# Attention and feed-forward in one kernel: a shorter lag of the exponentials, exponentials over two banks, and another order of the last matmuls

## The chip, the cores and the metric

The kernel runs on one core of a Trainium2 chip. The metric is the device time of one execution in microseconds. Five engines work side by side, each through its own list of instructions in order: TensorE (PE), ScalarE (ACT), VectorE (DVE), GpSimd (POOL) and SyncE (SP, which here issues the DMAs). PE writes its results to PSUM, which has eight banks of 512 fp32 values per partition; ACT and DVE read them there.

## The reference

A pre-LayerNorm block for 2048 tokens of 512 channels: attention with 32 heads of 16 channels, then a gated feed-forward network of 1792 channels.

```python
def _A_ref(x, wqkv, wo):
    qkv = ((x @ wqkv).reshape(B, S, 3, H, Dh)).transpose(2, 0, 3, 1, 4)
    q, k, v = qkv[0], qkv[1], qkv[2]
    scores = jnp.einsum("bhqd,bhkd->bhqk", q, k) * (Dh ** -0.5)
    p = _softmax(scores, axis=-1)
    o = jnp.einsum("bhqk,bhkd->bhqd", p, v)
    return o.transpose(0, 2, 1, 3).reshape(B, S, D) @ wo

def _B_ref(x, w_gate, w_up, w_down):
    return (_gelu(x @ w_gate) * (x @ w_up)) @ w_down

x = A_x
h = x + _A_ref(_layernorm(x), A_wqkv, A_wo)
h2 = h + _B_ref(_layernorm(h), B_w_gate, B_w_up, B_w_down)
```

Inputs and output are bf16, S = 2048, D = 512, H = 32, Dh = 16, F = 1792.

## The kernel before

**Units and steps.** Attention is cut into 64 units. A unit is one group of 256 query tokens (`gi`, 0 to 7) and one slot of four heads (`slot`, 0 to 7); the units of one token group follow each other, so a group lasts 8 units. A unit has 16 steps, and the main loop of the kernel (L1293) counts steps in `tick`. Each unit is gone through twice.

**First pass (p1): maxima.** `p1_pair` (L787) makes, in each step, the scores of 128 queries against 512 keys for two heads: two matmuls of 512 columns (L797) into two neighbouring PSUM banks. The pairs of banks alternate between 0, 1 and 2, 3 (for the first `DOUBLES` = 20 steps there are three pairs). `p1_consume` (L803) reduces both banks to maxima with one instruction on DVE, 128x2 from 128x1024 (L806). POOL combines the maxima of a unit: `negm_part` after steps 8 and 12 (L817 to L824), `negm_pre` after step 15 (L832 to L840), which writes the negated maximum in three bf16 pieces into ST. `negm_post` issues a DMA that transposes ST into STG (L846) and, `ADDX` = 4 steps later, lets POOL add STG to the unit's part of Q (L851): K has rows of ones, so the second pass gets score minus maximum out of the matmul.

**Second pass (p2): exponentials.** It begins `P2_START` = 16 + `LAGX` steps after the first pass of the same unit. `p2_tile` (L860) makes the transposed scores, 128 keys by 256 queries, two matmuls of 256 columns into one bank (L867), for two heads a step. `p2_consume` (L872) lets ACT take the exponential of the bank (128x512 fp32, L879) into one tile of a ring of 34 bf16 tiles, which lie in three areas (PTM 23, PTE 4, PTG 7). The second pass and the work below share banks 4 to 7, which `Banks` hands out. In one step the matmuls of the first pass and the first tile of the second form a group on PE: all waits of the group stand at its first instruction (`group_begin`, `group_end`, L124 to L147), so that the next maximum's matmuls also wait for what the tile waits for.

**Dense work.** Everything else on PE is a list of small items (`Dense`, L510) that gives the loop one piece in each step: projections to Q, K and V, the product with V (`item_pv`, L893), transposes and normalisation of its result (`item_ofin`; POOL takes the reciprocal with a power, L928, and multiplies, L932), the output projection (`item_oproj`, L994), the second LayerNorm (sums by ACT with L1005 and L1012, the rest on POOL, L1022 to L1036), and the feed-forward network (`item_gate`, `item_up`, `item_down`). Gate and up results are copied out of PSUM by ACT (`evac_act`, L641; by DVE, L630, once there are no maxima left); the gelu is a chain of POOL steps around a tanh on ACT (`gelu_chain`, L1045: L1062, L1063, L1064, tanh L1055, L1060, L1061, then L1114). POOL work goes through `PoolStream` (L594), which gives POOL a budget of about 1.19 us a step and holds costly operations back in some steps. Where a step has less dense work than two matmuls of 512 columns, `dummy` (L1283) fills it with matmuls whose result nobody reads.

**Steps without maxima.** After step 1023 the second pass still has 16 + `LAGX` steps, 24 here. They are taken two at a time: four tiles, each with its exponential, then dense work or dummies up to `FILL_2` = 4 units of 512 columns. The last token group's first three quarters of the output projection (`tail_a`, `tail_a2`) are made in these steps. Then `tail_b` (L1227) normalises the last unit (`tail_norm`, `tail_onT`), finishes the projection (L1237), takes the LayerNorm on DVE (L1240 to L1251), transposes (`tail_hnT`, L1213) and runs the last feed-forward block. `fill(n)` (L1176) puts n units of dense work or dummies on PE where a chain of other engines runs; `FILL_LN` is the one behind the LayerNorm. The down projections of the group before the last wait until then (`startable`, L504).

The scheduling is all done when the program is built: on the chip each engine only runs its list and waits on semaphores.

Of the kernel before, what the change touches and what calls it, by code (L numbers as in the profile page):

```python
# [223 lines left out]
LAGX = 8  # L224
PAUSE = 1
DOUBLES = 20
FILL_2 = 4
FILL_LN = 16
# [5 lines left out]
def bass_sequential_preLN__mha_block__geglu_ffn__prompt_kernel(nc, A_x, A_wqkv, A_wo, B_x, B_w_gate, B_w_up, B_w_down, out):  # L234
    dbg = None
    with ExitStack() as es:
# [264 lines left out]
        def startable(it, room):  # L501
            if it[0] is item_gate and par_busy[it[1][1] % 2] and room < 10:
                return False
            if it[0] is item_down and it[1][0] == GL - 1 and not force[0]:  # L504
                return False
            if it[0] is item_down and it[1][1] == 0 and not force[0]:
                return not gut_left.get(it[1][0], 0) and dense.now >= gut_last.get(it[1][0], 0) + 1
            return it[0] is not item_projT or not (qks_busy.get(("a", qk_n[0] % 4)) or qks_busy.get(("b", qk_n[0] % 2)))

        class Dense:  # L510
# [17 lines left out]
            def _start(self, item):  # L528
                genfn, a, est, nb = item
                if self.single:  # L530
# [63 lines left out]
        class PoolStream:  # L594
# [23 lines left out]
        ticking = [False]  # L618
        pool = PoolStream()
# [158 lines left out]
        for fn_ in qk_late:  # L778
            fn_()
        early = {0: [lambda: stats_dve(12), c2_rest], 1: [lambda: stats_dve(13), lambda: stats_dve(14), lambda: stats_act(15)], 2: [c2_dve, c3_rest],  # L780
                 5: [c3_act], 9: [lambda: w_order("q", 1, "act")], 11: [lambda: w_order("k", 1, "act")], 16: [lambda: w_order("q", 2, "act")],
                 18: [lambda: w_order("k", 2, "act")], 20: [lambda: w_order("q", 3, "act")], 22: [lambda: w_order("k", 3, "act")]}
# [59 lines left out]
        def negm_post(ui):  # L842
# [17 lines left out]
        def p2_tile(ui, j, gp, jj):  # L860
# [3 lines left out]
            m, g, b = j // 2, 2 * gp + jj, banks.take()  # L864
# [5 lines left out]
            return (b, m, g)  # L870

# [173 lines left out]
        def gelu_chain(par, dE):  # L1045
# [4 lines left out]
            def later(n):  # L1050
                if not force[0] and act_lag[0] > LAG_OP + 0.1 * n:
# [95 lines left out]
        def tail_a(b):  # L1147
# [9 lines left out]
            dense.add(tail_a2, front=True, est=4, not_before=dense.now + 2)  # L1157
            return 1

        def tail_a2(b):  # L1160
            gp = GL % 2
            for k in range(2):
                for hc in range(3):
                    P.op("pe", lambda e, k=k, hc=hc: e.matmul(pbank[:, k, :], OnT[:, k, hc, :], wo_sb[:, hc, :], start=(hc == 0), stop=False),
                         reads=[("OHa", 0), "wo"], writes=[("pb", k)], sig=False)
                    if hc == 1:
                        yield 2
                P.op("pe", lambda e, k=k: e.matmul(pbank[:, k, :], ident[:], g_h(GL, k), start=False, stop=False),
                     reads=["ident", ("h", gp, k)], writes=[("pb", k)], sig=(k == 1))
                if k == 0:  # L1170
                    yield 2
            a_done[0] = True
            return 2
        a_done = [False]
# [118 lines left out]
        while True:  # L1293
# [5 lines left out]
            if tick == P2_START - 4:  # L1299
# [107 lines left out]
```

## Time and profile before

| | |
|---|---|
| median of three runs | 1243.11 us (1242.97 to 1243.45) |
| profiled execution | 1243.15 us |
| its span, first to last instruction | 1241.40 us |
| granted clock of TensorE, mean | 0.997 |
| maxima (L806) | 1024, first starts at 14.66 us, last ends at 1184.92 us |
| exponentials (L879) | 2048 of 128x512, first starts at 46.46 us, last ends at 1211.31 us |
| first gate matmul of the last feed-forward block | 1219.97 us |

Busy time counts an engine from the start to the end of its instructions; where instructions of one engine overlap by their start and end, their mean duration is longer than the pitch at which they follow each other. A row of the timeline has the start, the time from the first start to the last end, engine, line, operation, output and inputs, shape and how many instructions are merged in it; in brackets stands the idle time before it and what ended that. "PEld" is the loading of weights on PE.

### The profile page before, as it was taken

The numbers are of one execution on the slowest core, as the hardware profiler recorded it, in microseconds if no ns is written. First come the engines' busy times: TensorE is split into PE (matmuls) and PEld (weight loads), VectorE is DVE, ScalarE is ACT, GpSimd is POOL, SyncE is SP. The second block draws the span as 40 slices with busy tenths as digits, with TensorE's granted clock in tenths as the row PEclk, the third lists the DMA queues.
The fourth block names the chain that finished last, engine by engine and source line by source line (L and its number), as shares of the span: only waits on it lengthen the run. The fifth ranks groups of instructions, "written<-read, shape, count | busy, mean of one in ns | idle before, by whom it ended". The sixth has DMA issues, their size and how long they took to land.

```text
span 1241.4 us, 31438 instructions
## 1 busy us (share of the span) xinstructions
PE 1137.8 (92%) x12680; PEld 437.8 (35%) x12680; DVE 1189.8 (96%) x1088; ACT 1199.9 (97%) x2464; POOL 764.3 (62%) x1540
## 2 busy tenths in 40 slices
PE   7999888899999999999999998999999999999998
PEld 3333222233333333333333333333333333333335
DVE  8999999999999999999999999999999999999923
ACT  7899999999999999999999999999999999999992
POOL 8647774467746765376645777367654766547760
PEclk9999999999999999999999999999999999999989
DMA  5101004300010000100010000100002000100000
GB/s 151 31 22 28 24 19 130 89 6 3 6 31 12 6 6 6 38 5 6 4 27 18 4 6 6 27 17 6 6 4 40 6 4 6 27 19 3 6 13 18
DMA packets 50800, 27.45 MB, mean 22 GB/s; under 512 B 36064, under 2 KB 49632, under 8 KB 50656
## 3 DMA queue, kind: packets, MB, share of 16 engines
q1 hardware_dynamic: 50656, 25.45, 8.0%
q8 instruction: 101, 1.65, 0.5%
q14 instruction: 43, 0.35, 0.1%
HBM read 11.80 MB, written 2.10 MB: 11 GB/s over the span
## 4 chain that ended last, share of the span: by engine, by line
DVE 58%; ACT 30%; PE 9%; POOL 2%; issue 1%; DMA 0%
DVE PM L806 57%; ACT PTM L879 17%; ACT PTG L879 5%; ACT PTE L879 3%; PE pbank L1122 2%; PE pbank L867 2%; PE pbank L797 1%; ACT th_sb L1055 1%; PE pbank L1072 1%; ACT g_sb L641 1%; ACT OnT L1012 1%; ACT u_sb L641 1%; PE pbank L739 1%; PE pbank L998 1%; PE pbank L676 1%
## 5 line engine op out<-in xcount | busy, mean ns | idle before, releaser
L806 DVE TENSOR_REDUCE PM<-pbank 128x2 f32<-128x1024 f32 x1024 | 1162.4, 1224 | 5.3 <-PE pbank L867 2.8
L879 ACT ACTIVATE PTM<-pbank 128x512 bf16<-128x512 f32 x1388 | 737.0, 669 | 4.7
L867 PE MATMUL pbank<-QT,KT 32*128 32x256 bf16 x4096 | 498.2, 273 | 9.7 <-ACT PTM L879 4.4
L797 PE MATMUL pbank<-KT,QT 32*128 32x512 bf16 x2048 | 394.2, 382 | 46.4 <-DVE PM L806 23.6
L1285 PE MATMUL pbank<-ones_bf,ident 128*128 128x512 bf16 x794 | 245.3, 384 | 28.1 <-ACT PTM L879 3.2
L797 PEld LDWEIGHTS pbank<-KT,QT 32*128 32x128 bf16 x2048 | 104.5, 91 | 392.7 <-DVE PM L806 170.3
L879 ACT ACTIVATE PTG<-pbank 128x512 bf16<-128x512 f32 x420 | 228.2, 660 | 1.1 <-PE pbank L867 0.3
L867 PEld LDWEIGHTS pbank<-QT,KT 32*128 32x128 bf16 x4096 | 164.5, 92 | 65.7 <-ACT PTM L879 36.8
L879 ACT ACTIVATE PTE<-pbank 128x512 bf16<-128x512 f32 x240 | 137.7, 667 | 1.9 <-PE pbank L867 1.1
L893 PE MATMUL pbank<-PTM,VA 128*17 128x256 bf16 x2776 | 125.8, 274 | 2.7 <-ACT PTM L879 1.2
L832 POOL TENSOR_TENSOR MX<-PM,MX 128x8 f32<-128x8 f32 x64 | 12.9, 202 | 163.9 <-DVE PM L806 163.9
L1285 PEld LDWEIGHTS pbank<-ones_bf,ident 128*128 128x128 bf16 x794 | 47.6, 97 | 131.4 <-ACT PTM L879 83.8
L928 POOL TENSOR_TENSOR LINV<-OAT,negone 128x16 f32<-128x16 f32 (+1 forms) x32 | 92.7, 2896 | 0.0
L893 PEld LDWEIGHTS pbank<-PTM,VA 128*17 128x17 bf16 x2776 | 60.1, 89 | 46.9 <-issue 29.1
L821 POOL TENSOR_TENSOR MX<-PM,MX 128x8 f32<-128x8 f32 x64 | 13.0, 203 | 101.5 <-DVE PM L806 101.5
L1072 PE MATMUL pbank<-hnT_l,wu_sb 128*128 128x256 bf16 x448 | 67.1, 276 | 3.1 <-ACT PTM L879 0.2
L1072 PE MATMUL pbank<-hnT_l,wg_sb 128*128 128x256 bf16 x448 | 66.9, 275 | 2.5
L1114 POOL TENSOR_TENSOR GUT<-th_sb,u_sb 128x512 bf16<-128x512 f32 x49 | 62.2, 1270 | 5.1 <-DVE u_sb L630 3.0
L1061 POOL TENSOR_TENSOR th_sb<-th_sb,g_sb 128x512 f32<-128x512 f32 x49 | 62.1, 1268 | 4.1
L1064 POOL TENSOR_TENSOR th_sb<-th_sb,g_sb 128x512 f32<-128x512 f32 x49 | 62.1, 1268 | 3.1
L1062 POOL TENSOR_TENSOR th_sb<-g_sb 128x512 f32<-128x512 f32 x49 | 51.0, 1041 | 18.8 <-ACT g_sb L641 18.8
L1122 PE MATMUL pbank<-wd_sb,GUT 128*128 128x512 bf16 x224 | 60.5, 382 | 0.6 <-ACT PTM L879 0.2
(149 smaller groups left out, 1077.3 us busy)
## 6 DMA issues: line engine op xcount, KB each, us to landing
QKS<-QKS SPq DMA_DIRECT2D x27, 112.0 KB, 2.2
x_sb<-in_A_x_dram SPq DMA_DIRECT2D x4, 512.0 KB, 5.6
xres<-in_A_x_dram SPq DMA_DIRECT2D x16, 128.0 KB, 2.2
out_dram<-out_sb SPq DMA_DIRECT2D x16, 128.0 KB, 1.8
wg_sb<-in_B_w_gate_dram SPq DMA_DIRECT2D x4, 448.0 KB, 5.0
wu_sb<-in_B_w_up_dram SPq DMA_DIRECT2D x4, 448.0 KB, 4.0
wd_sb<-in_B_w_down_dram SPq DMA_DIRECT2D x3, 512.0 KB, 6.4
STG<-ST SPq DMA_TRANSPOSE x64, 2.3
```

The source lines that it names most:

```text
L797: P.op("pe", lambda e, g=g, b=b: e.matmul(pbank[:, b, :], QT[32 * g:32 * g + 32, c, slot, 128 * qt:128 * qt + 128], KT[32 * g:32 * g + 32, ...
L806: P.op("dve", lambda e: e.tensor_reduce(out=PM[:, par, qt, kc, g:g + 2], in_=pbank[:, b:b + 2, :], axis=AX.X, op=ALU.max), reads=[("pb", b ...
L867: P.op("pe", lambda e, kt=kt, i=i: e.matmul(pbank[:, b, 256 * i:256 * i + 256], KT[32 * g:32 * g + 32, slot, 128 * kt:128 * kt + 128], QT[ ...
L879: P.op("act", lambda e, b=b, pi=pi: e.activation(out=PTt(pi), in_=pbank[:, b, :], func=ACT.Exp), reads=[("pb", b)], writes=[("PT", pi)], e ...
L893: P.op("pe", lambda e, g=g, kt=kt, pi=pi, i=i: e.matmul(pbank[32 * g:32 * g + 17, b, 0:256], VA[:, kt, 4 * slot + g, :], PTt(pi)[:, 256 * ...
L928: P.op("pool", lambda e: e.tensor_tensor(out=li, in0=oat4[:, :, :, 16], in1=negone[:, 0:8 * ns].rearrange("p (q h) -> p q h", q=2), op=ALU ...
L1061: o(1.27, lambda e: e.tensor_tensor(out=ts_, in0=ts_, in1=gs, op=ALU.mult), [("th", par), ("g", par)])], then=done)
L1064: o(1.27, lambda e: e.tensor_tensor(out=ts_, in0=ts_, in1=gs, op=ALU.mult), [("th", par), ("g", par)])], then=lambda: defer(TANH_LAG, lamb ...
L1072: P.op("pe", lambda e, dc=dc, fc=fc, i=i: e.matmul(pbank[:, b, 256 * i:256 * i + 256], w[:, dc, 128 * fc:128 * fc + 128], hT[:, dc, :], st ...
L1114: P.op("pool", lambda e: e.tensor_tensor(out=o_ap, in0=shp(ts_), in1=shp(us), op=ALU.mult), reads=[("th", par), ("u", par)], writes=o_keys ...
L1122: P.op("pe", lambda e: e.matmul(pbank[:, b, :], GUT[:, fc, 128 * k:128 * k + 128], wd_sb[:, fc, :], start=first, stop=last), reads=[("GUT" ...
L1285: P.op("pe", lambda e: e.matmul(pbank[:, b, :], ident[:], ones_bf[:, 0:512], start=True, stop=True), reads=["ident", "ones_bf"], writes=[( ...
```

## The change

- `LAGX` goes from 8 to 6: the second pass of a unit begins 22 steps after its first pass instead of 24. The weight reorderings of the projections (`w_order`) are put at steps 13, 15, 17 and 19 instead of 16, 18, 20 and 22, and the single-bank mode of the dense work begins at step `DOUBLES`, which is 20 before and after.
- The steps without maxima use three fixed pairs of neighbouring banks, and `p2_pair` takes one exponential of 128x1024 over both banks where the two ring tiles are neighbours in one area, and two of 128x512 where not. `FILL_2` goes from 4 to 5.
- POOL's multiplication by the reciprocal (L932) is held back in steps 1 and 2 of a unit while an add into Q is due; the tanh of the gelu chain waits longer for ACT to catch up, and waits while a gate or up item is in progress.
- The first down projection of the group before the last may start inside the loop.
- `tail_a2` is no longer an item of the dense work: its two halves stand in `tail_b`, in place of two fills of 3. `FILL_LN` goes from 16 to 13.

```diff
-LAGX = 8
+LAGX = 6
-FILL_2 = 4
-FILL_LN = 16
+FILL_2 = 5
+FILL_LN = 13
...
-            if it[0] is item_down and it[1][0] == GL - 1 and not force[0]:
+            if it[0] is item_down and it[1] == (GL - 1, 1) and not force[0]:
...
+                    if not flush and add_due[0] and qkv_over[0] and self.q[0][1].__name__ == 'mul' and dense.now % 16 in (1, 2):
+                        break
...
+            add_due[0] = True
             def add():
+                add_due[0] = False
                 pool.spend(0.7)
...
+        def p2_pair(ui, tiles):
+            pis = []
+            for (b, m, g) in tiles:
+                pi = pt_n[0] % NPT; pt_n[0] += 1
+                assert pi not in pt_busy, "PT ring too small"
+                pt_busy.add(pi)
+                pt_of[(ui, m, g)] = pi
+                pis.append(pi)
+            (b0, b1), (q0, q1) = [t[0] for t in tiles], pis
+            assert b1 == b0 + 1
+            if q1 == q0 + 1 and pt_tiles[q0][0] is pt_tiles[q1][0]:
+                o_ap = pt_tiles[q0][0][:, pt_tiles[q0][1]:pt_tiles[q0][1] + 2, :]
+                P.op("act", lambda e: e.activation(out=o_ap, in_=pbank[:, b0:b0 + 2, :], func=ACT.Exp), reads=[("pb", b0), ("pb", b1)], writes=[("PT", q0), ("PT", q1)])
+            else:
+                for b, pi in ((b0, q0), (b1, q1)):
+                    P.op("act", lambda e, b=b, pi=pi: e.activation(out=PTt(pi), in_=pbank[:, b, :], func=ACT.Exp), reads=[("pb", b)], writes=[("PT", pi)])
...
-                if not force[0] and act_lag[0] > LAG_OP + 0.1 * n:
+                if not force[0] and (act_lag[0] > LAG_OP + 0.02 * n or (n < 20 and dense.gen is not None and dense.cur in (item_gate, item_up))):
...
-            dense.add(tail_a2, front=True, est=4, not_before=dense.now + 2)
+            a_done[0] = True
...
+        def tail_a2(k):
             gp = GL % 2
...
+            for hc in range(3):
+                P.op("pe", lambda e, hc=hc: e.matmul(pbank[:, k, :], OnT[:, k, hc, :], wo_sb[:, hc, :], start=(hc == 0), stop=False),
+                     reads=[("OHa", 0), "wo"], writes=[("pb", k)], sig=False)
+            P.op("pe", lambda e: e.matmul(pbank[:, k, :], ident[:], g_h(GL, k), start=False, stop=False),
+                 reads=["ident", ("h", gp, k)], writes=[("pb", k)], sig=False)
...
-            fill(3)
             while not a_done[0]:
                 fill(1)
+            tail_a2(0)
             in_bank(tail_norm)
-            fill(3)
+            tail_a2(1)
             in_bank(tail_onT)
             fill(2)
...
-                    for b_ in (2, 3):
-                        banks.give(b_)
+                    own = dense.bank if dense.gen is not None else banks.free[0]
+                    other = own ^ 1
+                    banks.free = [other] if dense.gen is not None else [own, other]
+                    pairs = [0, 2, 10 - (own & 6)]
                 for d_ in (0, 1):
-                    for jj in (0, 1):
-                        t2l.append(p2_tile((t2 + d_) // 16, (t2 + d_) % 16, 1 - (tick + d_) % 2, jj))
-                        p2_consume((t2 + d_) // 16, t2l)
-                        t2l = []
+                    b_ = pairs.pop(0)
+                    pairs.append(b_)
+                    ui_, j_ = (t2 + d_) // 16, (t2 + d_) % 16
+                    p2_pair(ui_, [p2_tile(ui_, j_, 1 - (tick + d_) % 2, jj, b_ + jj) for jj in (0, 1)])
```

More of the change, by code (lines that the diff above doesn't have):

```diff
@@ L529, in _start @@
                 genfn, a, est, nb = item
+                self.cur = genfn
                 if self.single:
@@ L780, in bass_sequential_preLN__mha_block__geglu_ffn__prompt_kernel @@
         early = {0: [lambda: stats_dve(12), c2_rest], 1: [lambda: stats_dve(13), lambda: stats_dve(14), lambda: stats_act(15)], 2: [c2_dve, c3_rest],
-                 5: [c3_act], 9: [lambda: w_order("q", 1, "act")], 11: [lambda: w_order("k", 1, "act")], 16: [lambda: w_order("q", 2, "act")],
-                 18: [lambda: w_order("k", 2, "act")], 20: [lambda: w_order("q", 3, "act")], 22: [lambda: w_order("k", 3, "act")]}
+                 5: [c3_act], 9: [lambda: w_order("q", 1, "act")], 11: [lambda: w_order("k", 1, "act")], 13: [lambda: w_order("q", 2, "act")],
+                 15: [lambda: w_order("k", 2, "act")], 17: [lambda: w_order("q", 3, "act")], 19: [lambda: w_order("k", 3, "act")]}
         p1_ring = [0]
@@ L863, in p2_tile @@
             assert ui in q_ready
-            m, g, b = j // 2, 2 * gp + jj, banks.take()
+            m, g, b = j // 2, 2 * gp + jj, banks.take() if bank is None else bank
             for i in range(2):
@@ L1156, in tail_a @@
             P.op("dve", lambda e: e.tensor_copy(out=OnT[:, :, 0:3, :], in_=pt[:, 0:768].rearrange("p (k c s) -> p k c s", k=2, c=3)), reads=[("pb", b)], writes=[("OHa", 0), ("OH", 0), ("OH", 1)])
-            dense.add(tail_a2, front=True, est=4, not_before=dense.now + 2)
+            a_done[0] = True
             return 1
-        def tail_a2(b):
+        a_done = [False]
+        def tail_a2(k):
             gp = GL % 2
[L1162 to L1174, printed above, removed]
+            for hc in range(3):
[3 more added lines that the diff above has]
+                 reads=["ident", ("h", gp, k)], writes=[("pb", k)], sig=False)
         def fill(n):
```

5 lines of the change are left out of this document (3 added, 2 removed).

## The prediction

> **What bounds the kernel now.** I read the page first (busy time per engine, groups of instructions), then the timeline of VectorE (DVE), then the timelines of the last 80 us engine by engine, then stretches for the clock of TensorE (PE).
>
> ```profile
> PE 1137.8 (92%) x12680; PEld 437.8 (35%) x12680; DVE 1189.8 (96%) x1088; ACT 1199.9 (97%) x2464; POOL 764.3 (62%) x1540
> L806 DVE TENSOR_REDUCE PM<-pbank 128x2 f32<-128x1024 f32 x1024 | 1162.4, 1224 | 5.3 <-PE pbank L867 2.8
> ```
>
> DVE and ACT are both full, but DVE sets the pace: 1024 maxima of L806, back to back.
>
> ```profile
> 661.23 5.75 DVE L806 TENSOR_REDUCE PM<-pbank 128x2 f32<-128x1024 f32 x5 [0.29 <-PE pbank L867]
> 667.16 34.03 DVE L806 TENSOR_REDUCE PM<-pbank 128x2 f32<-128x1024 f32 x30 [0.17 <-PE pbank L867]
> ```
>
> The pitch is (34.03-1.22)/29 = 1.131 us a step. 1023 pitches and one duration make 1158.2 us; the first maximum starts at 14.66 and the last ends at 1184.92 (the DVE row of 3 from 1181.43), so 12.1 us of that stretch are waits. The timeline of DVE puts about 4 of them before 35 us (startup) and leaves some 7.7, of which some 7 come after 80 us in small pieces, near 0.95 us per 128 steps, such as the pauses at 661.23 and 667.16. There a down projection on PE (L1122) coincides with a square on ACT (L1012).
>
> From 1184.92 (call it T) ACT is the bound.
>
> ```profile
> 1187.61 7.05 ACT L879 ACTIVATE PTM<-pbank 128x512 bf16<-128x512 f32 x14
> ...
> 1202.95 0.60 ACT L879 ACTIVATE PTE<-pbank 128x512 bf16<-128x512 f32 x1 [1.10 <-PE pbank L867]
> ...
> 1205.33 2.06 ACT L879 ACTIVATE PTG<-pbank 128x512 bf16<-128x512 f32 x4 [0.31 <-PE pbank L867]
> 1207.25 4.06 ACT L879 ACTIVATE PTM<-pbank 128x512 bf16<-128x512 f32 x8
> ```
>
> The 48 exponentials without maxima start at T-0.2 and end at 1211.31 = T+26.39; they hold two tanh and waits of 1.1 and 0.31 us for PE, which ran at half clock then:
>
> ```profile
> 1192.50:1195.90 3.40, 3.19 (x40) 1.38 (x38) 0.98 (x2) 3.40 (x9) 3.23 (x4) 1.00 0.02 5
> 1195.90:1199.30 3.40, 2.22 (x15) 0.65 (x12) 0.30 (x1) 3.21 (x8) 3.23 (x5) 1.00 0.01 2
> 1199.30:1202.70 3.40, 3.36 (x20) 0.83 (x16) 0.00 (x0) 2.56 (x6) 3.32 (x4) 0.50 0.00 0
> ```
>
> (Columns: stretch, length, busy PE, PEld, DVE, ACT, POOL, clock, DMA.) The half clock follows a stretch in which PE was busy 2.22 of 3.40 us. After the last exponential 30.09 us remain to 1241.40: the normalisation of the last unit, the last LayerNorm, the last feed-forward block on PE.
>
> ```profile
> 1212.35 0.38 PE L1192 MATMUL pbank<-ident,OA 128*128 128x128 f32 x2
> ...
> 1218.44 0.61 PE L1213 MATMUL pbank<-ident,OnT 128*128 128x128 bf16 x8
> ...
> 1219.97 1.04 PE L1072 MATMUL pbank<-hnT_l,wg_sb 128*128 128x256 bf16 x8
> ```
>
> **The change, part by part.** Against the span of 1241.40; the profiled execution took 1243.15, 0.04 above the median.
>
> *Lag 8 to 6.* In the built order the steps without maxima fall from 24 to 22, so 4 exponentials move ahead of T. The single pitch is 0.478 us (fourteen from 1187.61 to the start of ACT's next row, a tanh, at 1194.30: 6.69/14). They start at step 22 instead of 24, where ACT was busy 3.24 of 4.00 us (44 to 48), and the reordering of weights (w_order) moves ahead of them into stretches of 2.69 to 3.33 busy of 4.00: covered there. Price if not: up to 4 x 0.48 = 1.9 us.
>
> *The price of the shorter lag.* The second pass of a unit needs the add of its maxima into Q (POOL L851), and the PE group that waits for it begins with the matmuls of the next maximum (L797). Unit 62:
>
> ```profile
> 1166.90 0.20 POOL L832 TENSOR_TENSOR MX<-PM,MX 128x8 f32<-128x8 f32 x1 [3.40 <-DVE PM L806]
> ...
> 1168.65 0.24 POOL L840 TENSOR_TENSOR ST<-R,ST 128x8 bf16<-128x8 f32 x1
> 1168.82 1.04 POOL L1062 TENSOR_TENSOR th_sb<-g_sb 128x512 f32<-128x512 f32 x1
> ...
> 1171.87 0.67 POOL L851 TENSOR_TENSOR QT<-QT,STG 128x256 bf16<-128x256 bf16 x1
> ...
> 1172.62 0.39 PE L797 MATMUL pbank<-KT,QT 32*128 32x512 bf16 x2
> ```
>
> Counted from the unit's last maximum (0.08 before L832 starts): ST is ready at 2.07, the add runs 5.05 to 5.73, and PE reaches step 22, the new deadline, at 5.80. With an idle POOL the add ends at 5.17 (the DMA lands at 4.5). PE may be 0.47 late before DVE stalls: a maximum starts 0.43 after its L797 (369.33 to 369.76 in the timelines), and step 22's maximum is due at 7 x 1.131-1.22 = 6.70, so L797 may start until 6.27. What the built order puts between ST and the add decides:
> - The reciprocal L928 (2.9 us), which stood there in nearly every odd unit (add end 6.26 in such units), now runs before the last maximum. With its three gelu steps (1.13+0.70+1.23 by their pitches) the add ends at 5.73. No stall.
> - In units 18 and 26, eight LayerNorm steps: 3.1 us by the pitches of L1022 to L1036 (0.30, 0.28, 0.28, 0.27, 0.66, 0.28, 0.33, 0.74); end 5.80. No stall.
> - In units 10, 34, 42, 50 and 58, twelve such steps: 4.25 us, add 6.26 to 6.93, PE at 7.0, 1.2 late; DVE loses 0.73, five times: **+3.7 us**. From below 0.4 each (2), above 1.1 (5.5) if the exponentials lag too.
>
> *The old pauses.* From the fourth token group on the down projection stands at steps 8 to 17 of 128, away from the squares at 46 and 49. The pauses of group 1, which has squares without a down projection, add up to about 0.3 us: I keep 0.35 of 0.95 us a cycle for seven cycles, 2.4 of 6.95: **-4.5 us**. Bounds: 0 (the same pauses elsewhere) and -7. Both parts move the last maximum to T' = T-0.8.
>
> *One exponential over two banks.* 22 pairs; as built 20 are joint and two fall back to singles where the ring tiles don't adjoin. No row has 128x1024 f32 in Exp. Nearest: L487, a copy of 128x1024 from PSUM, 1.02 us alone, two in 1.94, pitch 0.92. The other bound is the single's pitch with its second 512 elements at 1.2 per ns, 0.478+0.427 = 0.905. I take 0.91 against 2 x 0.478; all in all 20 x 0.045 = 0.9 us less, 0.7 to 1.0. The Trainium skill (ScalarE: Activation LUTs, "What ACT_TABLE_LOAD costs") gives 186 ns + 0.833 ns an element, less 93 ns overlap back to back: 520 ns for 512, 946 for 1024, so about 1.9 us saved, 1 us more than I count; the measured 0.478 for 512 already differs from it.
>
> *The stretch without maxima, from T'.* Pair 0 needs the banks of the second to last maximum, pair 1 those of the last: pair 1 runs from T'+0.4, pair 5 ends at T'+4.95. Pair 6 is the last unit's first and waits for its add (three gelu steps before it): end T'+5.74, then matmuls, exponential at T'+6.15; the one tanh left lies in that gap. From there 13 x 0.91 + 2 x 0.96 + 1.02 = 14.8: the last exponential ends at T'+20.9, against T+26.4: **-5.5 us**. PE hides below it: two steps need 8 scores (0.25 to 0.55) and 5 units of 0.216, some 1.6 of 1.82. If half clock comes, as before, add 1.3 to 2.4.
>
> *The end.* tail_a2 is now two blocks of 4 matmuls instead of fills of 3: the normalisation comes 0.22 and 0.08 later. FILL_LN 13 lets the last transposes start when hn is ready (L1251 ends at 1217.88, they started at 1218.44), and no down work remains before the first gate: it starts 8.26 after the last exponential instead of 8.66: **-0.4 us**, +0.3 to -0.7.
>
> Sum: 1241.4-0.8-5.5-0.4 = 1234.7 span; with 1.75 around it **1236.5 us**.
>
> **Rivals.**
> - *The loop runs clean* (0.15): the five late adds cost little, the old pauses go: T' = T-5, **1232**. For it: L797 has slack every step. Against: the twelve steps are in the order and their pitches hardly vary.
> - *The end stretch gives less* (0.14): PE idles about 1.3 us before pair 6, half clock follows, the loss of before is repeated: +1.3 to 2.4, with a costlier pair (0.956, none saved) +0.9: **1239.5**. For: one such stretch did it at 1195.90. Against: 2.2 us of its 3.4 remain dense.
> - *Half clock in the loop* (0.15), the other side: PE's 1.2 us wait at the five late units leaves about 2.1 busy of 3.4 us, less than the 2.22 that preceded half clock. Half clock lasted 6.8 us. A step's PE work (scores 0.43, values 0.55: 661.73 to 662.71) doubles to 1.96, 0.83 over the pitch, 3.5 steps: 2.9 us each, five times 14.5: **1251**; two of five make 1242, from three on it is slower than before. Against: at 18.30 to 21.70 PE was busy 2.29 of 3.40 and the clock stayed 1.00, and the five stretches would hold dense matmuls where that at 1195.90 held small ones. The Trainium skill (TensorE: Matmul & The Clock Gate, "What's actually happening") lets the clock fall after an idle window of 3.4 us; by it this rival would not occur, but here a window two thirds busy was enough.
> - The forecast itself has 0.56, with 1233 to 1239.5 as its own range.
>
> **How the numbers follow.** 0.2% is 2.5 us, about what can be told from no change: faster is below 1240.6, slower above 1245.6. Faster takes nearly all of the forecast, the clean loop and most of the smaller end (0.54+0.15+0.10 = 0.79); same takes what is left of the forecast and parts of the last two (0.02+0.03+0.04 = 0.09); slower the rest of half clock and a hundredth of the smaller end (0.12). The range goes from the lower part of the clean loop to three of five late units at half clock: 1231 to 1245, with about 0.07 left out below and 0.10 above.
>
> **What would show it.** Right: the last maximum ends near 1184, with pauses of about 0.7 us at units 10, 34, 42, 50, 58 released through L867's wait for POOL's add; 20 exponentials of 128x1024 of about 1.02 us; the last exponential some 21 us after the last maximum; 29.7 us from it to the end. Wrong: clock below 1.00 inside the loop, pauses in odd units (a DMA later than 4.5), or pairs that wait for PE.

## The result, and the profile after

The changed kernel takes 1250.56 us (median of 4 runs, 1249.67 to 1251.62), the kernel before 1243.28 us beside it (1242.97 to 1244.01): ratio 1.0058, 95% interval 1.0041 to 1.0075. The change makes the kernel slower by 7.3 us, where 6.6 us less were predicted. The profiled execution took 1251.62 us, with a span of 1249.9 us.

The page of the changed kernel: busy time per engine, the chain that ended last by engine, and two groups of instructions (busy time, mean ns | idle time before them and what ended it).

```profile
PE 1102.5 (88%) x12485; PEld 436.9 (35%) x12681; DVE 1191.7 (95%) x1086; ACT 1200.9 (96%) x2446; POOL 763.0 (61%) x1540
...
ACT 51%; DVE 29%; PE 9%; POOL 4%; issue 4%; DMA 2%; SPq 0%; POOLq 0%; DVEq 0%
...
L810 DVE TENSOR_REDUCE PM<-pbank 128x2 f32<-128x1024 f32 x1024 | 1165.8, 1212 | 15.5 <-PE pbank L873 11.2
...
L857 POOL TENSOR_TENSOR QT<-QT,STG 128x256 bf16<-128x256 bf16 x64 | 42.8, 668 | 41.0 <-DMA STG<-ST 40.9
```

The maxima (L810) wait 15.5 us instead of 5.3, 11.2 of it for the scores of the second pass (L873, before 2.8), and the chain, which before led for 58% of the span through DVE, now leads for 51% through ACT. The timeline of VectorE, two stretches in a steady part and the last maxima:

```profile
671.89 36.35 DVE L810 TENSOR_REDUCE PM<-pbank 128x2 f32<-128x1024 f32 x32 [0.51 <-PE pbank L873]
708.51 27.49 DVE L810 TENSOR_REDUCE PM<-pbank 128x2 f32<-128x1024 f32 x24 [0.26 <-PE pbank L873]
...
1186.96 11.65 DVE L810 TENSOR_REDUCE PM<-pbank 128x2 f32<-128x1024 f32 x10 [0.26 <-PE pbank L873]
```

The last maximum ends at 1186.96 + 11.65 = 1198.61 us, 13.7 later than the 1184.92 of before. The timeline of ScalarE from there:

```profile
1200.65 3.77 ACT L890 ACTIVATE PTM<-pbank 128x1024 bf16<-128x1024 f32 x4 [0.34 <-PE pbank L873]
1204.28 0.65 ACT L1078 ACTIVATE th_sb<-th_sb 128x512 f32<-128x512 f32 x1
1204.86 5.61 ACT L890 ACTIVATE PTM<-pbank 128x1024 bf16<-128x1024 f32 x6
1210.30 0.66 ACT L893 ACTIVATE PTM<-pbank 128x512 bf16<-128x512 f32 x1
...
1215.82 3.94 ACT L890 ACTIVATE PTM<-pbank 128x1024 bf16<-128x1024 f32 x4
```

The last exponential ends at 1219.76, 21.15 after the last maximum, and the span ends 30.14 later: 51.3 us for what took 56.5. So the tail gained 5.2 us and the loop lost 13.7.

Where the loop lost them follows from the starts of the 1024 maxima: what two starts are apart beyond 1.131 us is a wait. The table adds these waits up, by the place of the step in its token group of 128 steps (steps after 63 only; the first 64 stand alone):

| us of waits | first 64 | steps 0-39 | 40-67 | 68-99 | 100-127 | sum | last maximum ends |
|---|---|---|---|---|---|---|---|
| before | 5.5 | 0.0 | 5.3 | 1.1 | 0.1 | 12.0 | 1184.9 |
| changed | 5.1 | 3.7 | 5.9 | 5.5 | 5.4 | 25.6 | 1198.6 |
| lag 8, rest changed (e2) | 5.5 | 0.3 | 4.5 | 1.1 | 0.2 | 11.6 | 1184.7 |
| lag 6, other loop rules old (e4) | 5.1 | 2.7 | 5.8 | 4.6 | 5.6 | 23.8 | 1196.7 |
| values' products 2 later (e9) | 5.4 | 2.7 | 5.7 | 2.0 | 0.5 | 16.3 | 1189.8 |
| half tanh (e11) | 5.1 | 3.3 | 5.8 | 1.1 | 2.0 | 17.3 | 1190.7 |

Of the 13.6 us that the waits grew by, 9.7 stand in steps 68 to 127. There the changed kernel has a pair of pauses of 0.36 and 0.22 us at steps 86 and 89 and again at 118 and 121, in nearly every group; together they make some 7.3 of the 9.7 us. The other 2.4 are two single late adds, of unit 4 (steps 86 to 88 of group 0, 1.8 us) and of unit 53 (step 102 of group 6, 0.6 us). The places of the recurring pauses are those of the feed-forward items. ScalarE's timeline around one of them, the rows of exponentials left out (the pauses are those at 708):

```profile
688.41 0.63 ACT L1078 ACTIVATE th_sb<-th_sb 128x512 f32<-128x512 f32 x1
...
692.05 0.39 ACT L645 ACTIVATE OA<-pbank 128x256 f32<-128x256 f32 x1
...
694.22 0.67 ACT L645 ACTIVATE g_sb<-pbank 128x512 f32<-128x512 f32 x1
...
696.60 0.74 ACT L645 ACTIVATE u_sb<-pbank 128x512 f32<-128x512 f32 x1
...
699.94 0.83 ACT L645 ACTIVATE g_sb<-pbank 128x512 f32<-128x512 f32 x1
...
703.30 0.90 ACT L645 ACTIVATE u_sb<-pbank 128x512 f32<-128x512 f32 x1
...
705.91 0.75 ACT L1078 ACTIVATE th_sb<-th_sb 128x512 f32<-128x512 f32 x1
...
709.52 0.63 ACT L1078 ACTIVATE th_sb<-th_sb 128x512 f32<-128x512 f32 x1
...
710.99 0.41 ACT L645 ACTIVATE OA<-pbank 128x256 f32<-128x256 f32 x1
```

The same place with lag 8 (second run):

```profile
684.86 0.63 ACT L1078 ACTIVATE th_sb<-th_sb 128x512 f32<-128x512 f32 x1
...
686.34 0.41 ACT L645 ACTIVATE OA<-pbank 128x256 f32<-128x256 f32 x1
...
690.56 0.61 ACT L645 ACTIVATE g_sb<-pbank 128x512 f32<-128x512 f32 x1
...
692.95 0.67 ACT L645 ACTIVATE u_sb<-pbank 128x512 f32<-128x512 f32 x1
...
696.28 0.77 ACT L645 ACTIVATE g_sb<-pbank 128x512 f32<-128x512 f32 x1
...
699.62 0.88 ACT L1078 ACTIVATE th_sb<-th_sb 128x512 f32<-128x512 f32 x1
...
703.35 0.63 ACT L1078 ACTIVATE th_sb<-th_sb 128x512 f32<-128x512 f32 x1
...
704.82 0.41 ACT L645 ACTIVATE OA<-pbank 128x256 f32<-128x256 f32 x1
```

Between the two results of the values' products (OA) lag 8 has five copies and tanhs, the change six: one u more. (At the second place, between the OA of steps 103 and 120, it is six against four.) Each takes about 0.48 us (from its start to the next row's). ACT has 1.131 - 2 x 0.478 = 0.175 us a step to spare for them. From the first tanh to the end of the second OA the change's nine items take 4.0 us in 22.8, lag 8's eight 3.5 in 20.2; with two exponentials a step ACT's work exceeds the time by 0.5 us there and by 0.4 here. The cover is what PE and ACT are ahead by when a burst begins; the matmuls of a maximum run at most 0.57 us ahead of what it needs (from the start of L801 to that of L810 it is at most 1.00 us, and 0.43 where the maximum waits), and by the end of the burst nothing of that is left. A tenth of a microsecond decides between a pause and none, so such a count shows where to look and not more. Whether the bursts are the cause, or the late adds, or something else in the order, only the runs could tell.

One thing can be read from the trace beforehand. The step of the pause at 708.51 is the one at which the second pass of unit 36 begins and needs that unit's add. Here are the add, and TensorE up to the matmuls of that step's maximum:

```profile
706.24 0.67 POOL L857 TENSOR_TENSOR QT<-QT,STG 128x256 bf16<-128x256 bf16 x1 [0.36 <-DMA STG<-ST]
...
707.21 0.39 PE L873 MATMUL pbank<-QT,KT 32*128 32x256 bf16 x2 [0.23 <-ACT PTE L902]
...
707.53 0.61 PE L916 MATMUL pbank<-PTM,VA 128*17 128x256 bf16 x16
...
708.08 0.39 PE L801 MATMUL pbank<-KT,QT 32*128 32x512 bf16 x2
```

The add ended at 706.91, 1.17 us before TensorE came to the step. What had held it up, one step earlier, was a wait of 0.23 us for an exponential of ScalarE (L902). It is the same in nine of the twelve pauses of some 0.36 us: the add ends 5.45 to 5.54 us after the unit's last maximum, TensorE comes at 6.62 to 6.70. So these pauses are not late adds; that adds close to their deadline cost TensorE its lead at an earlier step is not excluded by it.

### The profile page after: what moved, and what is told of

It reads as the page before. It is cut to its first block, busy times and chain, and to the rows that moved or that the text cites. A ratio compares the mean times of both kernels' runs of the same rounds, so it can differ in the third digit from the quotient of the medians.

```text
span 1249.9 us, 31260 instructions
## 1 busy us (share of the span) xinstructions
PE 1102.5 (88%) x12485; PEld 436.9 (35%) x12681; DVE 1191.7 (95%) x1086; ACT 1200.9 (96%) x2446; POOL 763.0 (61%) x1540
## 4 chain that ended last, share of the span: by engine, by line
ACT 51%; DVE 29%; PE 9%; POOL 4%; issue 4%; DMA 2%; SPq 0%; POOLq 0%; DVEq 0%
ACT PTM L902 30%; DVE PM L810 28%; ACT PTG L902 8%; ACT PTE L902 5%; PE pbank L1145 2%; PE pbank L801 2%; ACT th_sb L1078 2%; ACT u_sb L645 2%; ACT g_sb L645 2%; PE pbank L873 2%; DMA STG<-ST 1%; PE pbank L1301 1%; PE pbank L1095 1%; POOL LINV L951 1%; ACT OA L645 1%
## 5 line engine op out<-in xcount | busy, mean ns | idle before, releaser
L810 DVE TENSOR_REDUCE PM<-pbank 128x2 f32<-128x1024 f32 x1024 | 1165.8, 1212 | 15.5 <-PE pbank L873 11.2
L902 ACT ACTIVATE PTM<-pbank 128x512 bf16<-128x512 f32 x1357 | 726.7, 688 | 11.1 <-PE pbank L873 6.3
L873 PE MATMUL pbank<-QT,KT 32*128 32x256 bf16 x4096 | 509.0, 273 | 14.0 <-ACT PTM L902 5.0
L801 PE MATMUL pbank<-KT,QT 32*128 32x512 bf16 x2048 | 394.9, 384 | 49.7 <-DVE PM L810 18.3
L1301 PE MATMUL pbank<-ones_bf,ident 128*128 128x512 bf16 x626 | 202.9, 384 | 53.7 <-ACT PTM L902 25.7
L801 PEld LDWEIGHTS pbank<-KT,QT 32*128 32x128 bf16 x2048 | 101.0, 91 | 385.4 <-DVE PM L810 133.2
L902 ACT ACTIVATE PTG<-pbank 128x512 bf16<-128x512 f32 x411 | 227.4, 679 | 2.5 <-PE pbank L873 1.0
L873 PEld LDWEIGHTS pbank<-QT,KT 32*128 32x128 bf16 x4096 | 167.5, 92 | 76.3 <-ACT PTM L902 40.1
L902 ACT ACTIVATE PTE<-pbank 128x512 bf16<-128x512 f32 x236 | 136.9, 687 | 3.0 <-PE pbank L873 2.0
L916 PEld LDWEIGHTS pbank<-PTM,VA 128*17 128x17 bf16 x2776 | 60.1, 90 | 48.2 <-issue 30.2
L857 POOL TENSOR_TENSOR QT<-QT,STG 128x256 bf16<-128x256 bf16 x64 | 42.8, 668 | 41.0 <-DMA STG<-ST 40.9
L821 POOL TENSOR_TENSOR MX<-PM 128x8 f32<-128x8 f32 x64 | 12.9, 202 | 71.3 <-DVE PM L810 70.3
```

What stands on the lines that cost most here:

```text
L801: P.op("pe", lambda e, g=g, b=b: e.matmul(pbank[:, b, :], QT[32 * g:32 * g + 32, c, slot, 128 * qt:128 * qt + 128], KT[32 * g:32 * g + 32, ...
L810: P.op("dve", lambda e: e.tensor_reduce(out=PM[:, par, qt, kc, g:g + 2], in_=pbank[:, b:b + 2, :], axis=AX.X, op=ALU.max), reads=[("pb", b ...
L873: P.op("pe", lambda e, kt=kt, i=i: e.matmul(pbank[:, b, 256 * i:256 * i + 256], KT[32 * g:32 * g + 32, slot, 128 * kt:128 * kt + 128], QT[ ...
L902: P.op("act", lambda e, b=b, pi=pi: e.activation(out=PTt(pi), in_=pbank[:, b, :], func=ACT.Exp), reads=[("pb", b)], writes=[("PT", pi)], e ...
L916: P.op("pe", lambda e, g=g, kt=kt, pi=pi, i=i: e.matmul(pbank[32 * g:32 * g + 17, b, 0:256], VA[:, kt, 4 * slot + g, :], PTt(pi)[:, 256 * ...
L1301: P.op("pe", lambda e: e.matmul(pbank[:, b, :], ident[:], ones_bf[:, 0:512], start=True, stop=True), reads=["ident", "ones_bf"], writes=[( ...
```

## The experiments

The theories at the start: A, the shorter lag costs the loop its time; B, the new rule for the tanh packs ScalarE. Then, under A: the adds of the maxima (A1) or the order of the work that the lag brings (A2). The expectations of e9 to e12 call the denser bursts B1, and lag 6 itself, with its adds just in time, B2.

**e1 to e4: which part of the change.** e1 is the change with only the tail's edits; e2 sets only the lag back; e3 only the rule for the tanh; e4 has lag 6 with the other loop rules old.

```diff
 e1: LAGX = 8, old tanh rule, old startable, old w_order, no rule for mul
 e2:
-LAGX = 6
+LAGX = 8
 e3:
-if not force[0] and (act_lag[0] > LAG_OP + 0.02 * n or (n < 20 and ... dense.cur in (item_gate, item_up))):
+if not force[0] and act_lag[0] > LAG_OP + 0.1 * n:
 e4: e1 with LAGX = 6 and the change's w_order
```

> Lag 8, old tanh rule, old order of weights: of the change only the steps without maxima (pairs of banks, joint exponentials) and the tail (fills, last products) are left. Both theories expect the loop of before (last maximum near 1184) and the new tail with 24 instead of 22 steps in it: the change's tail took 51.3 us from the last maximum to the end against 56.5, of which some 1.9 us belong to the four exponentials that the lag moves; so -3.3 us, about 1240 (1239 to 1241). If it stays at 1243, the shorter tail came from the lag alone.

> The change with the lag set back from 6 to 8, everything else of it kept, the new tanh rule too. Theory A, the shorter lag (with the order of the work that it brings) costs the loop its 13.7 us: the loop is back, last maximum near 1184, total about 1240. Theory B, the new rule for the tanh packs gates, ups and tanhs onto ScalarE: pauses of about 0.7 us at steps 85 to 89 and 117 to 121 of the 128 stay, total about 1248.

> The change with the old rule for when a tanh is put into ScalarE's queue, lag 6 kept. Theory A (the lag): the pauses at steps 85 to 89 and 117 to 121 stay, 1249 to 1251. Theory B (the tanh rule): they go, some 8.5 us of the 13.7, about 1242.

> The first run here (steps without maxima and tail of the change) with lag 6 and the weights' order that goes with it; old tanh rule, no rule for the products on GpSimd, old rule for the last down projections. Against that first run only the lag differs. Theory A: slower by the loop's 13.7 us less the 1.9 of the four exponentials, 1250 to 1252. Theory B: about 1242 (five late adds cost 3.3 us).

Measured: e1 1244.02 us, ratio 1.0008 (0.9999 to 1.0017); e2 1243.58, 1.0004 (0.9995 to 1.0012); e3 1250.7, 1.0061 (1.0049 to 1.0074); e4 1252.86, 1.0078 (1.0066 to 1.0091). B falls: with the old rule the pauses only stand elsewhere, at steps 83 and 115 (0.52 us each; not at 78 to 83 and 110 to 113, as the expectation of e6 below has it). A holds: e1 and e4 differ by the lag (and the weights' order) alone, and the last maximum by 11.7 us.

The 1240 expected of e1 and e2 was wrong by 4 us, and not for the loop. With lag 8 the last exponential ends 24.0 us after the last maximum (before 26.4), but the span ends 33.1 later, not 30.1. The timeline of TensorE in e2 says why:

```profile
1217.38 2.54 PE L1145 MATMUL pbank<-wd_sb,GUT 128*128 128x512 bf16 x11
1219.76 0.81 PE L1150 MATMUL pbank<-xres,ident 128*128 128x512 bf16 x3
1220.40 1.04 PE L1095 MATMUL pbank<-hnT_l,wg_sb 128*128 128x256 bf16 x8
```

Eleven matmuls of down projections and the residuals stand ahead of the first gate, behind the last transposes. In the change 14 of them ran in the steps without maxima; with lag 8 the built order has none of them there, and 30 fillers in their place (e17 below changes the rule that keeps them out). e4 against e3 prices the rule that lets the down projection start: 33.1 against 30.1 us, 3.0 us.

**e5, e6: the add sooner.** `ADDX` 4 to 2, with the new and the old tanh rule.

```diff
-ADDX = 4
+ADDX = 2
```

> The change with the add of the maxima placed two steps after the DMA's issue instead of four (lag 6 kept): GpSimd gets hardly any feed-forward or LayerNorm step between ST and the add, so that adds end near 5.15 us after the unit's last maximum in all units. Theory A1 (the late and just-in-time adds cost TensorE its lead, and the lead was what covered ScalarE's feed-forward items): late adds and the pauses at steps 85 to 89 and 117 to 121 go, 11 of the 13.7 us, total 1239 to 1241. Theory A2 (the shorter lag puts other work beside the feed-forward items, and the adds matter only where they are late): only the five 0.65 and a few more go, total about 1246 to 1247, pauses at 85 to 89 and 117 to 121 stay.

> As the run before, with the old tanh rule, in which the pauses stood at steps 78 to 83 and 110 to 113. A1: 1239 to 1241. A2: the pauses stay there, 1246 to 1247.

Measured: 1306.67 us, ratio 1.0504 (1.0488 to 1.0519), and 1314.97, 1.0578 (1.0563 to 1.0594). The adds did come sooner (most end 5.13 after the unit's last maximum), and the kernel lost 56 us: both theories missed what else the edit moves. Two groups of e5:

```profile
L857 POOL TENSOR_TENSOR QT<-QT,STG 128x256 bf16<-128x256 bf16 x64 | 42.7, 668 | 101.8 <-DMA STG<-ST 101.8
...
L1078 ACT ACTIVATE th_sb<-th_sb 128x512 f32<-128x512 f32 x49 | 35.0, 715 | 41.0 <-POOL th_sb L1087 41.0
```

GpSimd stands 101.8 us in front of the add instead of 41.0, since hardly anything is queued ahead of it; the gelu steps behind it come late, and the tanh, already in ScalarE's queue, waits 41.0 us for them (1.7 in the change) with the exponentials behind it. The mean clock fell to 0.972. The runs tell nothing between A1 and A2.

**e7, e10: the add later, with lag 8.** If a just-in-time add made the pauses, it should make them with lag 8 too.

```diff
 e7: lag 8 and
-ADDX = 4
+ADDX = 6
 e10: lag 8 and
+ADDX = 7
```

> The change with lag 8 and the add placed two steps later (six after the DMA's issue), so that the add is about as close to its deadline as with lag 6, while the order of work on ScalarE and TensorE is that of lag 8. A1: pauses of the loop come back, 5 us or more over the run with lag 8 (1243.6). A2: within 1 us of 1243.6.

> As the run with lag 8 and a later add, but one step later again: there the adds still ended 0.7 to 0.8 us ahead of their step; here GpSimd has up to another microsecond of work ahead of them, so that they end at the deadline or some tenths behind it. B1: at most 2 us over lag 8 (1243.6), from late adds alone, no pauses at steps 85 to 91 and 117 to 121 beyond 0.3. B2: pauses there and 1248 or more.

Measured: e7 1243.88 us, ratio 1.0004 (0.9995 to 1.0014), but its adds still ended some 0.8 us ahead of their step, so it decides nothing. e10: 1249.86, 1.0049 (1.0034 to 1.0064). In e10 the adds of most odd units end 8.07 us after the last maximum and PE reaches their step at 8.22 instead of 8.02. In groups 2 to 7 this cost 0.3 us a group (1.1 of waits instead of 0.8), with 0.06 us at steps 116 to 121; the rest of its 5.2 us in the loop came mostly from the first units, whose adds ended as late as 9.4, and from a stretch at half clock at 22.9 us. The total missed B1's number, but the pauses of the change did not appear: a just-in-time add alone does not make them.

**e8, e12: slack for TensorE, items further apart.**

```diff
 e8:
-                want = 2
+                want = 1 if p2_started else 2
 e12:
-LAG_START = 0.4
+LAG_START = 0.3
```

> The change with one filler matmul a step instead of two in the loop once exponentials run (TensorE's step shorter by 0.216 us where it has no other work; no part of the result is computed by them). If TensorE misses its lead only because the fillers leave it no time to win it back: pauses shrink by half or more, 1244 to 1247. If the pauses come from ScalarE alone: 1250, as the change. If the clock falls because TensorE is less busy: slower than 1255, clock rows of 0.50.

> The change with the start of a gate or up projection allowed only at a smaller planned backlog of ScalarE (0.3 instead of 0.4 us): items lie further apart, down projections later. B1: pauses at steps 85 to 91 and 117 to 121 shrink by half, some of it back elsewhere, 1244 to 1248. B2: as the change, 1250.

Measured: e8 1249.67 us, ratio 1.0051 (1.0036 to 1.0066); e12 1266.34, 1.0176 (1.0159 to 1.0193). In e8 the waits were 23.0 us instead of 25.6 and the pauses at steps 116 to 121 were 0.2 to 0.4 us in most groups instead of 0.6, but half clock came at seven places of the loop (in the change at two); inconclusive. So it stays open how much TensorE's own work in those steps adds to the pauses. In e12 the pauses at steps 84 to 91 went, and others came at steps 16 to 55 and 100 to 121: the items that were spread fell among other work, and the feed-forward came so late that the end after the last exponential took 41.7 us. The total missed both numbers; distance alone is no remedy.

**e9, e11, e13: the bursts.** e9 keeps lag 6 and with it the steps at which adds and scores are due, and puts the values' products where lag 8 has them, so that the built order of the feed-forward is lag 8's (in group 4 ScalarE's copies, tanhs and squares stand at the same steps as in e2, one for one). e11 takes time off ScalarE and leaves every order as it is, by leaving out the tanh of half the elements; e13 does the same with lag 8.

```diff
 e9:
-                while not force[0] and dense.now < P2_START + 16 * ui + 4 * p + 5:
+                while not force[0] and dense.now < P2_START + 16 * ui + 4 * p + 7:
...
-                dense.add(item_pv, t2 // 16, front=True, est=5, not_before=tick + PV_T[0])
+                dense.add(item_pv, t2 // 16, front=True, est=5, not_before=tick + PV_T[0] + 2)
 e11 (e13: with LAGX = 8):
-activation(out=ts_, in_=ts_, func=ACT.Tanh, scale=GC)
+activation(out=ts_[:, 0:256], in_=ts_[:, 0:256], func=ACT.Tanh, scale=GC)
```

> The change with lag 6, but the products with the values (and what is planned around them) two steps later, where lag 8 has them; the built order of gates, ups, tanhs and products in a group is then that of lag 8, and only the exponentials, their scores and the adds' deadline stand two steps earlier. Its stretch without maxima has 30 fillers and no down projection, and 32 more matmuls with values stand behind the last exponential: about 55 us from the last maximum to the end, as in the fourth run (54.2) and some more. Theory B1 (the two steps put the values' products and the feed-forward items closer together, one item more in each burst than ScalarE's and TensorE's slack takes): pauses fall to those of lag 8, last maximum near 1186, total 1242 to 1244. Theory B2 (lag 6 itself: adds just in time, scores two steps closer to the maxima): last maximum at 1195 or later, total 1252 to 1255.

> The change with the tanh of the feed-forward on 256 of its 512 elements (the other half is left without tanh): 0.2 us less on ScalarE for each of 49, in each burst two or three of them. If ScalarE's work in the bursts makes the pauses (B1): the 0.58 us pauses at steps 85 to 91 and 117 to 121 nearly go, 7 us or more less, 1242 to 1244. If TensorE or GpSimd makes them: 1249 to 1251.

> Control to the half tanh: the same cut (tanh on 256 of 512 elements, the rest without) in the change with lag 8 (1243.6 with the whole tanh). If the cut only helps where the bursts are too dense, it gains here at most the 1 to 1.5 us that the small pauses of lag 8 at steps 50 to 59 and 84 to 91 hold: 1242 to 1243.6. If a shorter tanh is worth 7 us anywhere: 1236.

Measured: e9 1247.92 us, ratio 1.0033 (1.0020 to 1.0046); e11 1242.88, 0.9996 (0.9986 to 1.0005); e13 1242.16, 0.9990 (0.9981 to 1.0000). The same place of VectorE's timeline in e11 (behind a late add at step 54) is one row, where the change had a break at 708:

```profile
668.66 66.86 DVE L810 TENSOR_REDUCE PM<-pbank 128x2 f32<-128x1024 f32 x59 [0.50 <-PE pbank L873]
```

A tanh shorter by 0.2 us, three in a burst of 0.58 us of pauses, took 7.7 us off the change and 1.4 us off lag 8. And with lag 6 kept, lag 8's order took 8.8 us off the loop (last maximum 1189.8; waits in steps 68 to 127 down from 10.9 to 2.5 us). Of e11's 3.1 us left in steps 68 to 127, 2.3 are the late adds of three units (4, 53 and 62). That settles the larger part: the bursts on ScalarE, which the two steps made denser, are what stops VectorE. e9 alone would not show it, since its order moves TensorE's and GpSimd's work too; e11 shortens ScalarE's work alone, and the recurring pauses go.

e9's loop stays 5.1 us behind lag 8's. Most of that stands in steps 0 to 41 (3.5 us of waits, 0.3 with lag 8), where the adds of units 15, 24 and 33 end late, the last with a stretch at half clock behind it; the add of unit 44 costs another 0.8. The five late adds of the change do not occur in e9, so its order moved late adds as well.

**e14, e15: loop and tail together.** e14 is e9's order up to unit 53 and the change's from there; e15 adds `ADDX` = 3.

```diff
-... + 4 * p + 5:
+... + 4 * p + (7 if ui < 54 else 5):
...
-not_before=tick + PV_T[0])
+not_before=tick + PV_T[0] + (2 if t2 // 16 < 54 else 0))
```

> The change with the values' products two steps later for units 0 to 53 only (the order of lag 8), and as the change from unit 54 on, so that one down projection of the last but one group stands in the steps without maxima again. Loop as in the ninth run (1189.8) and one group's bursts (1.2), tail as in the change (51.3): span 1242 to 1243, total 1243 to 1245. If loop and tail were not separate terms, the tail would be 54 or more.

> As the run before, and the add three steps after the DMA's issue instead of four. If the 5 us over lag 8 that the ninth run's loop kept are late adds: last maximum near 1187, total 1238 to 1241, faster than both kernels. If an add that GpSimd waits for delays the products, as in the fifth run: 1246 or more.

Measured: e14 1243.55 us, ratio 0.9999 (0.9990 to 1.0008), last maximum 1189.8, tail 51.3 as in the change: loop and tail are separate terms. e15: 1251.48, 1.0061 (1.0046 to 1.0076), the loss of e5 in small: GpSimd stands 53.6 us in front of the add (30.2 in e14), and 6.4 us of waits fall in the last group alone, with two stretches at half clock. That the 5 us of e9 are late adds was read from its trace; e15 could not confirm it.

**e16, e17: lag 8 with a better end.** e16 fills TensorE's two waits before the last transposes; e17 lets a down projection start in the steps without maxima even if values' products are due.

```diff
 e16: lag 8,
-FILL_LN = 13
+FILL_LN = 16
...
                 in_bank(tail_hnT, k)
+                if k == 0:
+                    fill(3)
 e17: lag 8,
-... and self.now + self.ready[0][2] + PAUSE - 1 <= lim)):
+... and (self.now + self.ready[0][2] + PAUSE - 1 <= lim or (dve_free[0] and self.ready[0][0] is item_down)))):
```

> The change with lag 8 and the down projections that stood behind the last transposes moved before and between them (16 fills instead of 13, and 3 between the two blocks of transposes). Work that TensorE did after hnT (11 down matmuls, 2.4 us) then lies in its two waits of 0.58 and 0.52: 1.1 us less than lag 8 (1243.6), 1242 to 1243. If the wait for hnT only moves: 1243.6.

> The change with lag 8, and one rule more: without maxima a down projection may start even if a product with values is due within its time. So 14 down matmuls and their residual stand in the steps without maxima (plan: steps 18 to 22 of the last 24) where the second run had fillers, and the 33.1 us from the last exponential to the end become the 30.1 of the change; the products with values that wait for it fit beside the last four exponentials. If loop and tail are separate terms: 1184.6 + 24.0 + 30.1 to 30.6, span 1238.7 to 1239.2, total 1240.4 to 1241, faster than before by 0.2 per cent. If the late products with values hold the end up: 1242 or more.

Measured: e16 1243.1 us, ratio 0.9997 (0.9987 to 1.0006), 31.8 us after the last exponential instead of 33.1. e17 1241.62, 0.9983 (0.9974 to 0.9992): faster than both kernels, by 2.3 us than before. TensorE in e17:

```profile
1203.82 1.47 PE L1145 MATMUL pbank<-wd_sb,GUT 128*128 128x512 bf16 x6
...
1205.78 1.24 PE L1145 MATMUL pbank<-wd_sb,GUT 128*128 128x512 bf16 x5 [0.16 <-issue]
...
1218.30 1.04 PE L1095 MATMUL pbank<-hnT_l,wg_sb 128*128 128x256 bf16 x8
```

The down matmuls stand beside the exponentials, the first gate comes 8.7 us after the last of them, and 30.15 us remain to the end. Its last maximum ends at 1185.0, its last exponential 24.6 later where 24.0 were expected; the total lies 0.6 us above the range expected.

## Why the prediction was wrong

**What held.** The late adds: five predicted at 0.73 us each, in units 10, 34, 42, 50 and 58; measured five of 0.65 at just those units. One of them, unit 42, on GpSimd and on VectorE:

```profile
813.38 0.23 POOL L844 TENSOR_TENSOR ST<-R,ST 128x8 bf16<-128x8 f32 x1
...
817.67 0.67 POOL L857 TENSOR_TENSOR QT<-QT,STG 128x256 bf16<-128x256 bf16 x1
```

```profile
818.91 6.88 DVE L810 TENSOR_REDUCE PM<-pbank 128x2 f32<-128x1024 f32 x6 [0.50 <-PE pbank L873]
```

Twelve LayerNorm steps stand between ST and the add, as the built order had them, and VectorE is idle for 0.50 us; by the starts the maximum comes 0.60 late and the one before it 0.05. In most odd units the add ends at 5.71 to 5.78, predicted 5.73, or sooner, with no pause of its own; units 15, 31 and 53 are the exceptions (below). The old pauses beside the squares: predicted to fall from 6.95 to 2.4 us; of the 5.9 in steps 40 to 67 the five late adds are 3.3, so 2.6 stayed. The stretch: the last exponential 21.15 us after the last maximum, predicted 20.9; two banks in one exponential follow at 0.907 us (six of them from 1204.86 to 1210.30), predicted 0.91. The weights' order cost nothing (first 64 steps 5.1 us, before 5.5). The end was 30.14 us, predicted 29.7: the first gate came 8.7 us after the last exponential, not 8.26, so the 0.4 us gain of that term did not come.

**What failed.** The step "Both parts move the last maximum to T' = T-0.8". Its two parts are about right in size; the sum lacks a term, and the last maximum came at T+13.7. The prediction treated the lag as the exponentials and the add's deadline, and moved the down projections; it did not price that the values' products move with the exponentials, by two steps, and that gates, ups and tanhs are planned around them. That order was there to be compared: one item more in one burst of a group, two in the other. The trace of before gave little sign of it, a pause of 0.08 us at step 90 of most groups, inside the sum that the prediction put down to squares. The missing term is the recurring pauses, some 7.3 of the 9.7 us in steps 68 to 127, and e9 and e11 show what it is.

The second term that the sum lacks is late adds beyond the five: 2.4 us in units 4 and 53, and 3.7 us in steps 0 to 39, mainly units 15 (2.3, of which 1.9 at half clock behind it) and 31 (0.5). In units 15, 31 and 53 the DMA took 3.7 to 3.9 us to land, which the prediction had named as a sign against it. In unit 4 GpSimd's work ahead of the add waited 2.07 us for another DMA.

**The rivals.** Half clock in the loop gave about the measured total (1251), but by another way: it came twice, behind the late adds of units 4 and 15 and not at the five late units, what it can have cost there is at most 2.8 us and not 14.5, two of the four executions show a mean clock of 1.000 and take 1249.67 and 1251.18, and e4, whose loop has no such window, still ends its last maximum at 1196.7. The number of this rival was right by chance. "The loop runs clean" and "the end stretch gives less" did not occur.

**Why the parts do not add up to a gain.** Taken alone, the tail's edits with lag 8 are worth nothing (e1, 1.0008): joint exponentials and a clock that stayed at 1.00 gained 2.3 us up to the last exponential, and the down projections behind it took 3.0. With lag 6 they gain 5.2: the steps without maxima are two fewer and end 3.0 us sooner after the last maximum, and 14 down matmuls fit into them (30.1 instead of 33.1). The first belongs to lag 6, whose order costs the loop more than that. For the second lag 6 is not needed in the whole loop: the change's order in the last units is enough (e14), and with e17's rule so is lag 8.

## What to carry to other kernels

A shift of one pass by two steps moves everything that is planned around it; compare the built order of every engine that is nearly full, burst by burst, and set each burst's work against the slack of its place, not against the mean. List recurrent pauses by their place and not only by their sum: here the old ones behaved as predicted, and the loss came at places that had next to none. An instruction queued nearer to its input in an in-order engine does not come sooner for nothing: what stood between was work, and what waits for that work stands in other queues.

## What the runs showed of the hardware that was not expected

Half clock followed stretches in which TensorE was still busy for 62 and for 44%. The stretches of 3.41 us in the changed kernel (length, busy PE, PEld, DVE, ACT, POOL, clock, DMA, GB/s):

```profile
114.30:117.72 3.42, 2.11 (x47) 1.11 (x46) 2.93 (x3) 2.54 (x6) 1.40 (x2) 0.98 0.12 34
117.72:121.13 3.41, 3.08 (x36) 0.87 (x34) 2.45 (x2) 2.42 (x5) 0.07 (x1) 0.52 0.02 5
121.13:124.54 3.41, 3.36 (x31) 1.22 (x28) 3.34 (x3) 3.33 (x8) 0.56 (x3) 1.00 0.00 0
...
319.10:322.52 3.42, 1.50 (x17) 0.52 (x22) 3.10 (x3) 1.90 (x5) 2.59 (x4) 0.98 0.00 0
322.52:325.93 3.41, 3.41 (x34) 1.12 (x34) 1.66 (x3) 2.76 (x7) 1.72 (x4) 0.52 0.02 5
```

Here it lasted one stretch each time. The kernel before had two in a row; this is its second, behind the one at 1199.30 that the prediction shows:

```profile
1202.70:1206.10 3.40, 3.40 (x25) 1.17 (x18) 0.00 (x0) 2.84 (x6) 1.70 (x2) 0.50 0.00 0
```

At least one busy stretch brings the full clock back by the Trainium skill (TensorE: Matmul & The Clock Gate, "What's actually happening"). The changed kernel agrees with one: 3.08 and 3.41 us busy, then 1.00. In the kernel before one did not do: 3.36 us of 3.40 were busy, a second stretch at half clock followed, and 1.00 came behind that.

The transposing DMA of the maxima does not always take the 2.3 us of its median from issue to landing. Unit 15 of the change, GpSimd and the DMA queue (SPq: from issue on), with nothing else in that queue from 312 to 322 us:

```profile
315.02 0.23 POOL L844 TENSOR_TENSOR ST<-R,ST 128x8 bf16<-128x8 f32 x1
...
319.04 0.67 POOL L857 TENSOR_TENSOR QT<-QT,STG 128x256 bf16<-128x256 bf16 x1 [0.89 <-DMA STG<-ST]
```

```profile
315.28 1.17 SPq L850 DMA_TRANSPOSE STG<-ST  x1
```

It took 3.7 us; the add ended 6.53 us after the unit's last maximum, and the second stretch at half clock above followed. In unit 33 of e14 it took 4.4, there with the output and two loads issued within 2 us behind it:

```profile
641.86 1.17 SPq L850 DMA_TRANSPOSE STG<-ST  x1
643.11 0.54 SPq L1165 DMA_DIRECT2D out_dram<-out_sb  x1
643.70 2.37 SPq L994 DMA_DIRECT2D xres<-in_A_x_dram  x2
```

What delays it stays open; no run tried it alone. With lag 8 the deadline of such an add is two steps, 2.3 us, later.
